# A transformer block with windowed attention and a gated feed-forward part: the last three attention units and the feed-forward part in a new order

## The chip, the cores and the metric

The kernel runs on one core of a Trainium2 chip. The metric is the device time of one execution in microseconds. The core has a matrix engine (PE; its weight loads are shown as PEld), a vector engine (DVE), an activation engine (ACT), a general engine (POOL) and a synchronisation engine (SP), which here issues nearly all DMAs. Each engine works through its own instructions in the order in which they were written; engines wait for one another by semaphores. An engine whose next instruction has to wait does nothing else meanwhile. Matrix products are accumulated in PSUM, which has eight banks of 128 x 512 fp32 values.

## The reference

The input x has 2048 rows of 512 columns. All data are fp32, and the kernel keeps fp32 accuracy by splitting most operands into a high and a low part and adding three products.

```python
mod = (silu(c) @ w_mod)                 # six rows of 512: sa, ca, ga, sb, cb, gb
h = layernorm(x) * (1 + ca) + sa
q, k, v = h @ wqkv                      # 32 heads of 16
scores = q k' / 4, masked to the 256 keys up to and with the query
x = x + ga * ((softmax(scores) @ v) @ wo)
h = layernorm(x) * (1 + cb) + sb
x = x + gb * ((silu(h @ w1) * (h @ w3)) @ w2)      # 1792 inner columns
```

## The kernel before, in words

**Units of the attention.** The 32 heads are taken in 8 groups of four, the 2048 rows in 4 blocks of 512. A unit u is one group and one block (`g, b = divmod(u, 4)`), so there are 32 units, and units 28 to 31 are the last group on the four blocks. The work on a unit has three parts. `unit_a` makes queries and keys: twelve products on PE (line 481), the evictions and splits (lines 487 to 499), and then three pairs of copies (`rows`, line 504) that put them into `ring`, from which scores are read. `unit_b` finds the row maxima: 16 score products (line 537), a masked maximum of each on DVE (`top`, line 544), two small DVE instructions that form `mr` from the maxima (`parts`, lines 552 and 554), a transposition on PE (`turn`, line 560), an eviction (line 565) and a copy of these rows into `ring` (line 569). `unit_c` makes the scores again, transposed and now with the maxima subtracted (line 855), and with one of several ways of masking: DVE merges (line 873) and POOL selections (line 883), or a second PE product (line 858). ACT takes the exponential (lines 867 and 876). The values are multiplied on PE (line 816), and the result is evicted (line 923) and stored in DRAM (line 926).

**After the attention.** The sums of the softmax are read back and inverted (`o_sums`, line 1196), the outputs are read back, scaled and split (`o_part`, lines 1214 to 1226), and `o_proj` multiplies by wo (line 1238), whose gated copy `load_wo` reads and splits with four casts on ACT and four subtractions on POOL (lines 1170, 1092 and 1093). Layer norm, transpositions and splits follow. The feed-forward part runs over two halves of the rows and seven pairs of 128-column blocks of the inner dimension; it uses a Strassen form with seven products in place of eight (line 1502, evictions at lines 1525 to 1546), splits its result (lines 1574 and 1577) and multiplies by w2 (line 1596), adding into x1 (line 1601). The weights of each pair are read by `load_w` (line 1296) into one of two sets of buffers and split into high and low parts on ACT and on DVE or POOL (lines 1092 and 1093). The split of wo, the weights and other splits share those two lines.

**What sets the order.** Up to time TS = 232, in a time scale of 8 per unit, the attention's operations are issued in the order of times written by hand (table X: an operation of a unit has the unit's start plus an offset). Operations from TS on are not issued in that order. They are given, with everything that follows the attention, to a list schedule (`Sched.deal`): these are mainly parts of the last three or four units, and all maxima work of the last unit. The list schedule goes through an imagined run. Each engine takes the ready operation with the smallest key; an operation is ready when those it depends on are done by the assumed lengths, not before its earliest time `est`. An engine may wait up to `LOOK[engine]` for an attention operation with a smaller key. It also hands out the eight banks. What it deals out is only the order of issue on each engine. Real dependences are kept by semaphores whatever the list assumes.

The assumed lengths of products by columns are `MM`. `PEM` and `PEA` are the extra time assumed until PE sees the result of ACT, DVE or POOL. The key of an attention operation is its hand time in microseconds plus an entry of `OFF`, less 1000; keys of other operations come from `K`. Of these, `wo` is the key of the wo loads, `n` the parts of a block that must be there before its first out-projection product, `o` the blocks' out-projection keys, `w` an addition to the keys of the weight loads, `fl` the key distance between pairs of the feed-forward part, `te` an anchor of its keys, and `by`, `be`, `su`, `sr` and `sw` name the engine, DVE or POOL, of each multiplication and subtraction. `wo`, `n` and the others are tuned numbers without another meaning.

A dependence is known to the list only if an operation states it by name. In the kernel before, scores of line 537 state the copies into `ring` only for units under 3 (`rq if u < 3 else []`): the copies of the last unit are issued by hand order before the list begins, so the list knows no operation that writes them. Earliest times of attention operations are set by

```python
o.att, o.est = True, max(0.0, us(t)) if t < TS + 4 else 0.0
```

so an operation with a hand time below 236 has an earliest time, and one above has 0 unless something that it depends on is later.

Of the kernel before, what the change touches and what calls it, by code (L numbers as in the profile page):

```python
# [55 lines left out]
NU = NQ * NB  # L56
# [9 lines left out]
MM = {512: 0.228, 384: 0.175, 320: 0.148, 256: 0.121, 128: 0.062}  # L66
# [221 lines left out]
def us(t):  # L288
# [13 lines left out]
PEA = 0.11  # L302
LOOK = dict(PE=0.17, ACT=0.56, DVE=0, POOL=0.48, SP=2.26, NIL=0.0)
# [3 lines left out]
OFF = (-32.4, 1.9, 31.8, -10.9, -41.3, -73.5, -71.5, -77.4, -34.7, -2.4, -93.5, -48.6, -6.7, -60.6, -31.7,  # L307
# [12 lines left out]
K = dict(off=OFF, be=(('DVE', 'DVE'), ('POOL', 'DVE'), ('POOL', 'DVE'), ('DVE', 'POOL'), ('POOL', 'POOL'),  # L320
         ('POOL', 'POOL'), ('POOL', 'DVE')), hr=2.131, de=2.436, wo=-5.452, x1=27.702, xb=-20.166, xl=-57.124,
         os=-30.972, ol=(-283.199, -169.889, -117.309, -7.043), pl=(-256.514, 34.596, -186.064, -72.727),
         pe=(-72.047, -51.379, -87.785, -5.093), o=(-209.809, 195.543, 313.113, 92.985), n=(3, 3, 3, 1),
         w0=41.734, l2=-43.794, f=5.37, fl=6.37, by=((('DVE', 'DVE'), ('POOL', 'DVE'), ('POOL', 'POOL'),
         ('DVE', 'POOL')), (('DVE', 'POOL'), ('DVE', 'DVE'), ('POOL', 'POOL'), ('POOL', 'DVE')), (('DVE',
         'DVE'), ('POOL', 'DVE'), ('DVE', 'DVE'), ('DVE', 'DVE')), (('DVE', 'DVE'), ('POOL', 'POOL'), ('DVE',
         'DVE'), ('DVE', 'DVE'))), w=-0.289, dn=1.69, ds=0.072, l3=-28.825, sw=('POOL', 'POOL', 'POOL',
         'POOL'), su=(('DVE', 'DVE', 'POOL', 'DVE'), ('POOL', 'POOL', 'DVE', 'POOL'), ('DVE', 'DVE', 'DVE',
# [3 lines left out]
def block_kernel(ctx: ExitStack, tc: tile.TileContext, x, wqk, wv, wo, w13, w2, c, crow, wmod, wmodt, out):  # L332
# [715 lines left out]
    for t, _, fn, kind, use in ops:  # L1048
        if t < TS and use and len(use) == 4 and use[3] in n:
            bk = use[1][0]  # L1050
            bk.i = ("st", "mx").index(use[3]) * 3 + n[use[3]] % 3
            bk.tile = take, bk.i
            n[use[3]] += 1
    sch = Sched(free, take, [], [])
    for t, _, fn, kind, use in last:
        reads, writes, occ = use[:3]
        eng = KINDS[kind][0]
# [585 lines left out]
    n = 0  # L1643
# [88 lines left out]
```

## Time and profile before

| quantity | us |
|---|---|
| median of three runs (lowest, highest) | 962.61 (962.32, 962.68) |
| time of the profiled execution | 960.54 |
| its span, from the first instruction to the last | 958.8 |
| PE busy | 940.2 |
| DVE busy | 730.2 |
| ACT busy | 549.0 |
| POOL busy | 531.6 |

The granted clock of PE is 0.988 on the mean over the span, where 1 is full speed. Products are pipelined, so the busy time of PE says where it was empty rather than how well it was used. In a timeline each row gives the start, the length, the engine, the line, the operation with what it writes and reads, the count of merged instructions and, in brackets, the idle time of that engine just before and what ended it. If several things were waited for, the one that ended last by the profile is named. Units are not named in the trace; a unit's work is recognised by its order.

### The profile page before, as it was taken

The numbers are of one execution on the slowest core, as the hardware profiler recorded it, in microseconds if no ns is written. First come the engines' busy times: TensorE is split into PE (matmuls) and PEld (weight loads), VectorE is DVE, ScalarE is ACT, GpSimd is POOL, SyncE is SP. The second block draws the span as 40 slices with busy tenths as digits, with TensorE's granted clock in tenths as the row PEclk, the third lists the DMA queues.
The fourth block names the chain that finished last, engine by engine and source line by source line (L and its number), as shares of the span: only waits on it lengthen the run. The fifth ranks groups of instructions, "written<-read, shape, count | busy, mean of one in ns | idle before, by whom it ended". The sixth has DMA issues, their size and how long they took to land.

```text
span 958.8 us, 17155 instructions
## 1 busy us (share of the span) xinstructions
PE 940.2 (98%) x5322; PEld 725.6 (76%) x5322; DVE 730.2 (76%) x2054; ACT 549.0 (57%) x1247; POOL 531.6 (55%) x738
## 2 busy tenths in 40 slices
PE   9999999999999999998899999999999999999998
PEld 6668767777777776775688778888888888888886
DVE  7976789898989898988667695766679765566545
ACT  3333787878787877776669854433446343433330
POOL 8611686878687777774643775268556422222320
PEclk7999999999999999999899999999999999999999
DMA  9611354444454444345793664576555532222102
GB/s 316 209 57 35 109 176 148 147 152 145 148 178 144 149 144 148 133 137 183 223 257 127 198 204 154 190 252 220 162 164 191 166 99 89 71 65 82 36 23 88
DMA packets 81702, 141.90 MB, mean 148 GB/s; under 512 B 10570, under 2 KB 23242, under 8 KB 81612
## 3 DMA queue, kind: packets, MB, share of 16 engines
q1 hardware_dynamic: 81180, 140.29, 45.4%
q8 instruction: 42, 0.69, 0.3%
q10 hardware_dynamic: 432, 0.53, 0.2%
q14 instruction: 48, 0.39, 0.1%
HBM read 85.99 MB, written 34.61 MB: 126 GB/s over the span
## 4 chain that ended last, share of the span: by engine, by line
PE 83%; DVE 6%; POOL 4%; DMA 3%; issue 2%; ACT 1%; SPq 0%; ACTq 0%; POOLq 0%; DVEq 0%
PE st L1502 10%; PE mx L1502 9%; PE pj L481 7%; PE st L855 7%; PE mx L537 7%; PE po L816 7%; PE mx L1596 6%; PE st L1596 5%; PE po L1502 4%; PE mx L655 3%; PE pj L1502 2%; PE mx L1238 2%; PE st L655 2%; PE po L1596 2%; PE pj L1596 2%
## 5 line engine op out<-in xcount | busy, mean ns | idle before, releaser
L544 DVE CUSTOM_DVE_ANT_0 junk<-mx,mskq 128x384 bf16<-128x384 f32 (+2 forms) x487 | 244.0, 527 | 29.4 <-PE mx L537 27.9
L855 PE MATMUL st<-ring 100*128 100x384 f32 (+2 forms) x488 | 148.2, 345 | 0.6 <-ACT pt L876 0.4
L537 PE MATMUL mx<-ring 96*128 96x384 f32 (+1 forms) x487 | 146.0, 341 | 1.9 <-DMA ring<-qk 1.0
L883 POOL TENSOR_SCALAR_AFFINE_SELECT pt<-pt 128x256 f32<-128x256 f32 x268 | 108.6, 408 | 62.1 <-ACT pt L876 51.9
L481 PE MATMUL pj<-hT,wq 128*128 128x512 f32 x384 | 133.9, 407 | 0.0
L876 ACT ACTIVATE pt<-st 128x256 f32<-128x256 f32 x263 | 94.2, 386 | 37.5 <-DVE st L873 29.2
L1546 POOL TENSOR_TENSOR t<-t,t 128x512 f32<-128x512 f32 x28 | 41.0, 1463 | 134.1 <-DVE t L1534 133.4
L537 PEld LDWEIGHTS mx<-ring 96*128 96x128 f32 x487 | 88.8, 189 | 32.4 <-DVE mt L544 21.7
L855 PEld LDWEIGHTS st<-ring 100*128 100x128 f32 x488 | 91.6, 191 | 18.6 <-issue 6.7
L816 PE MATMUL po<-pt,vS 128*17 128x256 f32 (+2 forms) x1408 | 97.6, 390 | 2.9 <-POOL pt L883 2.5
L499 POOL TENSOR_TENSOR qk<-qkr,qk 128x512 fp32r<-128x512 f32 x64 | 83.2, 1300 | 15.6 <-ACT qkr L487 15.3
L873 DVE COPY_PREDICATED st<-later,st 128x128 f32<-128x128 uint8 x263 | 71.0, 291 | 14.0 <-PE st L855 10.7
L481 PEld LDWEIGHTS pj<-hT,wq 128*128 128x128 f32 x384 | 71.6, 191 | 7.2 <-DVE hT L650 0.7
L1093 POOL TENSOR_TENSOR w<-w,w 128x512 fp32r<-128x512 f32 (+2 forms) x35 | 55.8, 1607 | 33.4 <-ACT w L1092 33.4
L816 PEld LDWEIGHTS po<-pt,vS 128*17 128x17 f32 x1408 | 32.7, 97 | 48.0 <-issue 20.8
L1534 DVE TENSOR_TENSOR t<-mx,t 128x512 f32<-128x512 f32 x54 | 36.9, 687 | 35.4 <-PE mx L1502 33.1
L1502 PE MATMUL st<-b,w 128*128 128x512 f32 x240 | 60.1, 390 | 1.1 <-ACT t L1541 1.1
L900 POOL TENSOR_SCALAR_AFFINE_SELECT sm<-sm 128x256 f32<-128x256 f32 x109 | 41.9, 406 | 27.2 <-ACT sm L890 23.1
L1502 PE MATMUL mx<-b,w 128*128 128x512 f32 x228 | 56.8, 390 | 0.1
L867 ACT ACTIVATE pt<-st 128x384 f32<-128x384 f32 (+2 forms) x109 | 45.7, 434 | 13.8 <-DVE st L863 12.3
L1502 PEld LDWEIGHTS st<-b,w 128*128 128x128 f32 x240 | 45.0, 188 | 10.9 <-ACT t L1541 1.5
L1534 DVE TENSOR_TENSOR t<-st,t 128x512 f32<-128x512 f32 x35 | 24.1, 688 | 36.2 <-PE st L1502 32.5
(339 smaller groups left out, 2139.1 us busy)
## 6 DMA issues: line engine op xcount, KB each, us to landing
ring<-qk SPq DMA_DIRECT2D x192, 128.0 KB
o_dr<-os SPq DMA_DIRECT2D x32, 256.0 KB
w<-wsum SPq DMA_DIRECT2D x14, 512.0 KB
w<-w2g SPq DMA_DIRECT2D x14, 512.0 KB
jb<-in_w SPq DMA_DIRECT2D x24, 256.0 KB
wraw<-in_w SPq DMA_DIRECT2D x7, 768.0 KB
w<-wraw SPq DMA_DIRECT2D x14, 384.0 KB
e<-in_w SPq DMA_DIRECT2D x18, 256.0 KB
```

What stands on the lines that cost most here:

```text
L481: nc.tensor.matmul(v["ps"], WQ[g][w][:, n // 3], hTp(i, n // 3, b * BT, BT), start=(n == 0), stop=(n == 3 * KC - 1))
L499: nc.gpsimd.tensor_tensor(out=v[n], in0=v["raw"], in1=v[1].bitcast(F32), op=ALU.subtract)
L537: nc.tensor.matmul(v[i][:, :n], queries(NS, a, gq, 1), keys(NS, hh, a, k0, gq + 1 - k0), start=True, stop=True)
L544: nc.vector.tensor_tensor_reduce(out=junk[:, :n], in0=v[i][:, :n], in1=mskq[:, 3 * P - n:], scale=1.0, scalar=-3e38, op0=ALU.add, op1=ALU. ...
L816: nc.tensor.matmul(po[32 * i:32 * i + DH + 1, qb * P:(qb + nq) * P], vS[:, kb, 4 * g + i], pts[i // 2][:, i % 2, c0:c0 + nq], start=first, ...
L855: nc.tensor.matmul(ps[:, :nq], keys(NM, hh, a, kb, 1), queries(NM, a, kb, nq), start=True, stop=not plus)
L873: nc.vector.copy_predicated(ps[:, 0], later, ps[:, 2])
L876: nc.scalar.activation(pt_of(j, a)[:, hh, :2], v[j, a, hh][:, :2], AF.Exp, scale=SCALE)
L883: nc.gpsimd.affine_select(out=pt[:, :, 2 * m], in_=pt[:, :, 0], **w)
L1502: nc.tensor.matmul(ps(bk), WT[s, n][w][:, col], BB[t, k][r], start=start and c == 0, stop=stop and c == 5, skip_group_check=True)
L1534: return nc.vector.tensor_add(o, x, y)
L1596: nc.tensor.matmul(ps(bk), tiles[hk + (h,)][:, i * P:(i + 1) * P], w2_of(last, y, f), start=(m == 0), stop=(m == 5))
```

## The change

The change has four parts. First, a place-holder operation on the queue NIL, which issues nothing, is added to the list: it writes the name `("keys", 31)` and has the earliest time 1.9. Scores of line 537 of units from 3 on now read `("keys", u)`, so that the list holds the last unit's scores back until 1.9 us after its start; the other units' names have no writer and hold nothing back. The index into `OFF` is moved by one, since the place-holder comes first. Second, the assumed product lengths are set anew, and so are `PEA` and the entries PE, ACT, POOL and SP of `LOOK`. Third, all 206 entries of `OFF` are new. Fourth, all numbers of `K` are new, with the engines of many multiplications and subtractions. All four splits of wo stay on POOL.

```diff
-MM = {512: 0.228, 384: 0.175, 320: 0.148, 256: 0.121, 128: 0.062}
+MM = {512: 0.2303, 384: 0.177, 256: 0.124, 128: 0.07}
...
-PEA = 0.11
-LOOK = dict(PE=0.17, ACT=0.56, DVE=0, POOL=0.48, SP=2.26, NIL=0.0)
+PEA = 0.05
+LOOK = dict(PE=0, ACT=0.57, DVE=0.0, POOL=1.87, SP=0.93, NIL=0.0)
...
-OFF = (-32.4, 1.9, 31.8, -10.9, -41.3, -73.5, -71.5, -77.4, -34.7, -2.4, -93.5, -48.6, -6.7, -60.6, -31.7,
...
+OFF = (-49.5, -12.1, -22.4, -33.6, -56.0, -86.7, -88.5, -93.2, -17.6, 12.1, -94.0, -56.8, -33.7, -64.4, -78.4,
...
-         ('POOL', 'POOL'), ('POOL', 'DVE')), hr=2.131, de=2.436, wo=-5.452, x1=27.702, xb=-20.166, xl=-57.124,
-         os=-30.972, ol=(-283.199, -169.889, -117.309, -7.043), pl=(-256.514, 34.596, -186.064, -72.727),
-         pe=(-72.047, -51.379, -87.785, -5.093), o=(-209.809, 195.543, 313.113, 92.985), n=(3, 3, 3, 1),
-         w0=41.734, l2=-43.794, f=5.37, fl=6.37, by=((('DVE', 'DVE'), ('POOL', 'DVE'), ('POOL', 'POOL'),
...
-         'DVE'), ('DVE', 'DVE'))), w=-0.289, dn=1.69, ds=0.072, l3=-28.825, sw=('POOL', 'POOL', 'POOL',
...
+         ('DVE', 'POOL'), ('DVE', 'POOL')), hr=21.549, de=1.941, wo=-21.362, x1=28.573, xb=-29.268,
+         xl=-116.162, os=-27.898, ol=(-190.566, -166.456, -108.194, -61.649), pl=(-220.589, 37.55, -68.89,
+         -99.113), pe=(-60.146, -15.682, -95.487, -36.215), o=(-234.765, 94.893, 305.699, 215.681), n=(2, 1,
+         1, 2), w0=44.978, l2=-60.842, f=17.513, fl=5.731, by=((('POOL', 'POOL'), ('POOL', 'DVE'), ('POOL',
...
+         'DVE'), ('DVE', 'DVE'), ('DVE', 'DVE'))), w=20.278, dn=1.62, ds=-0.071, l3=-47.032, sw=('POOL',
...
-            at(t0 + y["mx"][i], lambda i=i: scores(i, bk[i]), "scores", (rq if u < 3 else [], [bk[i]], MM[n], "mx"))
+            at(t0 + y["mx"][i], lambda i=i: scores(i, bk[i]), "scores", (rq if u < 3 else [("keys", u)], [bk[i]], MM[n], "mx"))
...
     sch = Sched(free, take, [], [])
+    sch.op("NIL", lambda: None, 0.0, 0.0, [], [("keys", NU - 1)]).est = 1.9
...
-        o = sch.op(eng, fn, occ, us(t) + K["off"][len(sch.ops)] - 1000, reads, writes, mode=int(kind == "values"))
+        o = sch.op(eng, fn, occ, us(t) + K["off"][len(sch.ops) - 1] - 1000, reads, writes, mode=int(kind == "values"))
```

More of the change, by code (lines that the diff above doesn't have):

```diff
@@ new lines @@
+OFF = (-49.5, -12.1, -22.4, -33.6, -56.0, -86.7, -88.5, -93.2, -17.6, 12.1, -94.0, -56.8, -33.7, -64.4, -78.4,
[13 rows of a table added]
+K = dict(off=OFF, be=(('DVE', 'DVE'), ('POOL', 'POOL'), ('DVE', 'POOL'), ('POOL', 'DVE'), ('DVE', 'POOL'),
+         ('DVE', 'POOL'), ('DVE', 'POOL')), hr=21.549, de=1.941, wo=-21.362, x1=28.573, xb=-29.268,
+         xl=-116.162, os=-27.898, ol=(-190.566, -166.456, -108.194, -61.649), pl=(-220.589, 37.55, -68.89,
+         -99.113), pe=(-60.146, -15.682, -95.487, -36.215), o=(-234.765, 94.893, 305.699, 215.681), n=(2, 1,
+         1, 2), w0=44.978, l2=-60.842, f=17.513, fl=5.731, by=((('POOL', 'POOL'), ('POOL', 'DVE'), ('POOL',
+         'DVE'), ('DVE', 'DVE')), (('POOL', 'DVE'), ('POOL', 'DVE'), ('DVE', 'POOL'), ('DVE', 'DVE')),
+         (('DVE', 'DVE'), ('DVE', 'POOL'), ('POOL', 'DVE'), ('DVE', 'DVE')), (('POOL', 'DVE'), ('POOL',
+         'DVE'), ('DVE', 'DVE'), ('DVE', 'DVE'))), w=20.278, dn=1.62, ds=-0.071, l3=-47.032, sw=('POOL',
+         'POOL', 'POOL', 'POOL'), su=(('DVE', 'POOL', 'DVE', 'DVE'), ('DVE', 'DVE', 'POOL', 'POOL'), ('DVE',
+         'DVE', 'POOL', 'DVE')), sr=(('POOL', 'DVE', 'POOL', 'DVE', 'DVE', 'DVE', 'DVE', 'POOL', 'POOL',
+         'DVE', 'DVE'), ('DVE', 'DVE', 'DVE', 'DVE', 'POOL', 'DVE', 'DVE', 'DVE', 'POOL', 'POOL', 'POOL')),
+         te=45.488)
```

6 lines of the change are left out of this document (removed), and 25 rows, old and new, of the table OFF.

## The prediction

> **What bounds the kernel now.** I read the page first, then the busy time in stretches of 24 us, and then the two stretches that were not full.
>
> ```profile
> span 958.8 us, 17155 instructions
> PE 940.2 (98%) x5322; PEld 725.6 (76%) x5322; DVE 730.2 (76%) x2054; ACT 549.0 (57%) x1247; POOL 531.6 (55%) x738
> ...
> 432.00:456.00 24.00, 19.91 (x139) 12.11 (x131) 21.05 (x85) 14.45 (x40) 11.62 (x21) 0.93 0.60 181
> 456.00:480.00 24.00, 21.86 (x182) 15.60 (x186) 14.56 (x36) 17.28 (x48) 15.01 (x24) 0.86 0.77 227
> 528.00:552.00 24.00, 22.88 (x109) 18.81 (x108) 14.88 (x31) 20.45 (x35) 18.64 (x16) 1.00 0.62 203
> 576.00:600.00 24.00, 24.00 (x110) 19.86 (x109) 13.11 (x19) 9.45 (x15) 11.70 (x14) 1.00 0.49 154
> 600.00:624.00 24.00, 24.00 (x113) 19.95 (x112) 16.30 (x23) 11.00 (x18) 7.41 (x9) 1.00 0.55 187
> 912.00:936.00 24.00, 24.00 (x106) 19.70 (x106) 12.30 (x19) 8.10 (x14) 5.14 (x4) 1.00 0.07 23
> 936.00:960.00 24.00, 18.75 (x83) 15.06 (x81) 11.51 (x18) 1.27 (x2) 0.00 (x0) 1.00 0.23 88
> ```
>
> The columns of a stretch are its length, the busy time of PE, PEld, DVE, ACT and POOL, the granted clock, the DMA share and GB/s. TensorE (PE) is the bound: full at clock 1.00 in a feed-forward stretch such as 600 to 624. It loses 4.09 us of idle at 432 to 456, 2.14 at 456 to 480 and 1.12 at 528 to 552; the last stretch holds the closing additions and stores. The clock falls below 1.00 only in the two stretches around 456, where the order written by hand ends and the list schedule begins. So I looked at those microsecond by microsecond, with the same columns:
>
> ```profile
> 441.00:442.00 1.00, 0.75 (x5) 0.40 (x3) 1.00 (x5) 0.70 (x4) 0.93 (x3) 1.00 0.57 197
> 442.00:443.00 1.00, 0.00 (x0) 0.00 (x0) 1.00 (x3) 0.09 (x1) 0.95 (x3) 1.00 0.63 195
> 443.00:444.00 1.00, 0.00 (x0) 0.01 (x1) 0.06 (x1) 1.00 (x3) 0.57 (x2) 1.00 0.26 76
> 444.00:445.00 1.00, 0.98 (x4) 0.80 (x4) 0.54 (x2) 0.08 (x1) 0.24 (x1) 0.70 0.78 236
> 447.00:448.00 1.00, 1.00 (x10) 0.43 (x2) 0.37 (x4) 0.00 (x0) 0.00 (x0) 0.60 0.69 172
> 455.00:456.00 1.00, 0.00 (x0) 0.00 (x0) 1.00 (x5) 0.00 (x0) 0.95 (x2) 1.00 1.17 254
> 459.00:460.00 1.00, 1.00 (x4) 1.00 (x5) 1.00 (x2) 0.27 (x1) 1.00 (x1) 0.50 0.43 95
> 464.00:465.00 1.00, 1.00 (x5) 1.00 (x5) 0.50 (x2) 1.00 (x4) 0.69 (x2) 0.56 0.65 207
> ```
>
> There are two holes in PE, and a half clock behind each. A clock of 0.70 at 444 to 445 and 0.60 at 447 to 448 puts the first half-clock time at about 444.4 to 447.8, 3.4 us, of which 1.7 are lost; the second one runs to about 464.9, and from 459.0, where PE is busy again, 5.9 us at half speed lose 2.95.
>
> Next, who ends the holes, from the timeline:
>
> ```profile
> 439.85 1.92 SPq L504 DMA_DIRECT2D ring<-qk  x3
> 441.20 0.55 PE L855 MATMUL st<-ring 100*128 100x384 f32 x2
> 444.02 0.41 PE L537 MATMUL st<-ring 96*128 96x384 f32 x1 [2.27 <-ACT pt L876]
> 444.46 0.56 DVE L544 CUSTOM_DVE_ANT_0 junk<-st,mskq 128x384 bf16<-128x384 f32 x1 [1.40 <-PE st L537]
> 446.46 0.55 DVE L544 CUSTOM_DVE_ANT_0 junk<-pj,mskq 128x384 bf16<-128x384 f32 x1
> 447.06 0.18 DVE L552 SCALAR_TENSOR_TENSOR mr<-mt,zero 128x16 fp32r<-128x16 f32 x1
> 447.27 0.17 DVE L554 SCALAR_TENSOR_TENSOR mr<-mt,mr 128x16 fp32r<-128x16 f32 x1
> ...
> 456.40 2.49 POOL L1093 TENSOR_TENSOR wo<-wo,wo 128x512 fp32r<-128x512 f32 x2
> 456.48 0.84 PE L816 MATMUL po<-pt,vS 128*17 128x384 f32 x8 [1.81 <-POOL pt L883]
> 456.92 0.79 DVE L552 SCALAR_TENSOR_TENSOR mr<-mt,zero 128x16 fp32r<-128x16 f32 x1
> 457.74 1.18 DVE L554 SCALAR_TENSOR_TENSOR mr<-mt,mr 128x16 fp32r<-128x16 f32 x1
> 458.98 0.40 PE L560 MATMUL mx<-ident,mr 128*32 128x128 f32 x1 [1.65 <-DVE mr L554]
> ```
>
> The first hole (2.27 us) ends with a score of line 537. In the kernel before, a score of the last unit from the seventh on has the earliest time 0 in the list schedule and reads nothing, so the schedule may put it at its very start. The trace shows five row maxima (L544) from 444.46 to 446.46 and then the two mr instructions of the last but one unit. That unit had only three maxima left by its times (scores 13 to 15), so two of the five belong to the last unit, and a score of it stood at the head of PE. Its rows cannot have been there: their last copy was issued at about 441.2 and ended issuing at 441.77, and the chain of waits gives 2.29 us to such a copy:
>
> ```profile
> 439.26 2.29 DMA ring<-qk
> ```
>
> 441.2 + 2.29 is 443.5, near the start at 444.02. The ACT instruction that the wait is put down to fits too, so the DMA as its cause is my reading, not the profile's. The second hole is a chain on DVE: all sixteen maxima of the last unit, the two mr instructions, then the transposition on PE at 458.98, whose rows the remaining scores need.
>
> **The change part by part.** No instruction of computation is added or removed; what is new is the order on every engine from about 441 on, and which of DVE and POOL does some splits. The new operation on the queue "NIL" issues nothing.
>
> *The landing time.* The list's time 0 lies near 441.1 (its first PE score, planned at 0.30, is the second of the pair at 441.20), so 1.9 means 443.0, half a microsecond before the estimate 443.5. PE can now first take the two open scores of the last but one unit, and DVE their maxima and a third one: three maxima of 0.50 each (the first and the fifth start at 444.46 and 446.46: 2.00 / 4), 1.5 us, of which 1.4 fit into the 1.40 that DVE waited ahead of 444.46. The DVE chain to the transposition, 444.46 to 458.98, thus gets 1.4 shorter. The bounds are 0 (the new order puts another late operation at the head) and 2.27 (nothing waits).
>
> *The two mr instructions* took 0.79 + 1.18 = 1.97 at 456.92 and only 0.18 + 0.17 = 0.35 at 447.06. In the slow case the POOL was at a subtraction for wo from 456.40 to 458.89. The change moves wo from key -5.5 to -21.4, ahead of more of its rivals, and there is room for it:
>
> ```profile
> 448.66 0.60 ACT L923 ACTIVATE os<-po 128x512 f32<-128x512 f32 x1 [4.58 <-PE po L816]
> 450.45 0.88 POOL L883 TENSOR_SCALAR_AFFINE_SELECT pt<-pt 128x256 f32<-128x256 f32 x2 [6.21 <-ACT pt L876]
> 452.37 2.18 ACT L1092 ACTIVATE wo<-wo 128x512 fp32r<-128x512 f32 x4
> 453.07 2.52 POOL L1093 TENSOR_TENSOR wo<-wo,wo 128x512 fp32r<-128x512 f32 x2 [1.75 <-ACT wo L1092]
> ```
>
> ACT idles 4.58 us and POOL 6.21 before 450.5, while the four casts and four subtractions need 2.18 and 2.52 + 2.49. I take it that they move up and the mr pair falls to 0.35: a gain of 1.6. Bounds: 0, and 1.6. The Trainium skill, SBUF — State Buffer, section "SBUF: two separate sides", says that DVE with two SBUF inputs and GpSimd exclude each other from a shared port pair for a whole instruction; the slow pair agrees. By that rule the 1.6 is won only if no such POOL instruction is running just then; if one is, the sum stands at 1.4. The list schedule itself counts no such conflict for the mr pair, so a repetition of the slow rows is a rival below.
>
> *The first half clock* (1.7) should go with the first hole, but PE then merely reaches the second hole earlier, since DVE sets that one's end: I count 0 for it, with 1.7 as the bound. The same holds for the idle time of the first hole itself.
>
> *The values' wait* (1.81 at 456.48, behind POOL's wo work) and *the second half clock* (2.95) I keep at 0: the new order of keys does not say what PE finds to do at 455. If out-projection products are ready then (the parts waited for before the first product of a block go from 3, 3, 3, 1 to 2, 1, 1, 2), both go: bound 4.76. The other side of starting a block on fewer parts is that PE, which issues in order, stands behind a part that lands late; one landing like the 2.29 above is the bound, -2.3.
>
> *Product lengths, look-ahead, feed-forward keys.* Lengths go from 0.228 to 0.2303 for 512 columns; that costs no time by itself, only other choices. From 576 to 936 PE is full before but for 0.06 us at most in a stretch (first and last stretch above), so only a loss is possible there, priced with the rivals; up to it, the waits behind line 1541 could go:
>
> ```profile
> PE st L1502 <- ACT t L1541: 1.4, 2, 1.1
> ```
>
> I count 0, bound 1.4.
>
> *Sum.* 1.4 + 1.6 = 3.0 earlier at the transposition; PE is busy from there on but for about a microsecond, so the end moves with it. The profiled execution took 960.54 us, 1.74 above its span; 960.54 - 3.0 = 957.5. The three timed runs have the median 962.61, 2.07 above the profiled one, so the forecast is 962.61 - 3.0 = 959.6. With every bound on the good side the sum is 1.4 + 1.6 + 4.76 + 1.4 + 1.7 = 10.9, hence 951.7.
>
> The Trainium skill, TensorE: Matmul & The Clock Gate, section "HAM oscillation — how this bites in real kernels", speaks of PE idle gaps above about 3.4 us as those that cost the clock. Here 2.27 us and 1.81 + 1.65 us were enough, so I go by the trace; by the rule the two half clocks would not have come from these holes, and the good bound would shrink by 4.65 to 956.4.
>
> **The rivals.** *More is won:* the transposition comes 3.0 earlier and the second hole is filled as well. Then the 1.81 and the 2.95 go too: 3.0 + 4.76 = 7.8, time 954.8. For it: DMA, ACT and POOL have room around 448. Against it: the four wo subtractions are not the last step, loads of o and of the sums come behind them in a DMA share of 0.9 to 1.17.
>
> *The POOL still blocks:* only the 1.4 comes, time 961.2, within what a measurement of this kernel can tell from no change (about 0.2%, 1.9 us). For it: the list schedule does not count the conflict, and the slow pair above shows it. Against it: wo is moved away from there.
>
> *Weights late, the slower side.* The key of a pair's weight loads moves from 0.3 below to 20.3 above its base, so loads and splits now yield to much other work. The narrowest lead that I found before:
>
> ```profile
> 669.03 2.87 POOL L1093 TENSOR_TENSOR o<-o,o 128x1024 fp32r<-128x1024 f32 x1
> 681.94 1.53 PE L1502 MATMUL pj<-b,o 128*128 128x512 f32 x6
> ```
>
> Split done at 671.90, first product at 681.94: 10.0 us. A key is a rank, not a time, but if loads came later by more than 10.0, PE would stand for the rest. Midway between 10 and the full shift of 20.6 that is 5.3 idle and about 1.7 of half clock, less the 3.0 won: 4.0 slower, 966.6. Against it: POOL and ACT are at 31% and 46% in the stretch 600 to 624.
>
> *The change does not do what it says:* if the first hole came from the ACT instruction alone, the 1.4 falls and the 1.6 may stay: 961.0, counted with no change.
>
> **How the numbers follow.** Forecast 0.34; more 0.25; no difference (the POOL blocks, or the rows were not the cause) 0.19; slower, by late weights or by a part that lands late, 0.22. The first two are faster by over 0.2%: 0.59. The predicted time is 959.6. Below 952.5 lies only what needs nearly all good bounds at once (0.07), above 966.5 the upper half of the late-weight case (0.11); the range is 952.5 to 966.5. The faster cases alone span 952.5 to 960.7.
>
> **What will show it.** Right: no hole above 1 us near 442 to 444, scores of the last unit after about 443.5, an mr pair of 0.35 us and the transposition of line 560 near 456, clock 1.00 at 444 to 448. The forecast rather than "more" holds if PE still idles over 2 us ahead of that transposition with a half clock behind it. Wrong: a hole of the same size at the boundary that ends on ACT or DVE; the mr pair again above 1 us beside a POOL subtraction; idle time of PE ahead of line 1502 or 1238 after 480, ended by a weight split or a load; a longer end than the last four microseconds of before.

## The result, and the profile after

The changed kernel took 957.1 us in the median of four executions (956.48 to 957.99), the kernel before beside it 962.64 (962.32 to 965.44): ratio 0.9935, interval 0.9909 to 0.9960. In a later comparison on another chip it was 956.23 against 964.64, ratio 0.9924 (0.9904 to 0.9944). It is faster by 5.5 to 8.4 us; 3.0 was forecast. The profiled execution took 957.99 us, 1.7 above its span of 956.3.

The profiles start unequal. The last two products of the order written by hand (line 855 before, 857 after; both kernels issue the same up to there) begin at 441.20 before and at 442.85 after. So I count from these two products, "the last pair", to the end of the span: 517.6 us before, 513.4 after, 4.2 less.

The changed kernel's stretches of 24 us; columns as in the prediction:

```profile
432.00:456.00 24.00, 21.88 (x157) 12.59 (x155) 23.35 (x93) 15.42 (x42) 14.42 (x25) 1.00 0.60 178
456.00:480.00 24.00, 22.47 (x188) 15.41 (x185) 12.83 (x39) 18.44 (x50) 14.95 (x24) 0.93 0.89 253
528.00:552.00 24.00, 23.54 (x112) 19.35 (x111) 18.21 (x32) 21.25 (x35) 18.59 (x15) 1.00 0.61 208
576.00:600.00 24.00, 24.00 (x108) 19.78 (x107) 13.63 (x20) 10.31 (x17) 12.65 (x14) 1.00 0.52 165
```

PE's idle time in the first three went from 4.09 + 2.14 + 1.12 = 7.35 to 2.12 + 1.53 + 0.46 = 4.11, and the clock in the first two from 0.93 and 0.86 to 1.00 and 0.93. The feed-forward part is as full as it was. The timeline of the changed kernel:

```profile
442.85 0.55 PE L857 MATMUL st<-ring 100*128 100x384 f32 x2
443.41 0.44 PE L539 MATMUL st<-ring 96*128 96x384 f32 x1
443.96 1.27 PE L818 MATMUL po<-pt,vS 128*17 128x384 f32 x16
...
453.39 0.62 PE L539 MATMUL mx<-ring 96*128 96x384 f32 x2 [0.30 <-ACT pt L869]
454.42 0.45 PE L539 MATMUL mx<-ring 96*128 96x384 f32 x1 [0.40 <-ACT pt L878]
455.29 1.28 POOL L1096 TENSOR_TENSOR wo<-wo,wo 128x512 fp32r<-128x512 f32 x1
455.37 0.84 PE L818 MATMUL po<-pt,vS 128*17 128x384 f32 x8 [0.33 <-POOL pt L885]
458.64 1.28 POOL L1229 TENSOR_TENSOR qk<-qk,qk 128x512 f32<-128x512 f32 x1
459.59 0.36 DVE L554 SCALAR_TENSOR_TENSOR mr<-mt,zero 128x16 fp32r<-128x16 f32 x1
459.99 0.32 DVE L556 SCALAR_TENSOR_TENSOR mr<-mt,mr 128x16 fp32r<-128x16 f32 x1
460.48 0.27 PE L562 MATMUL mx<-ident,mr 128*32 128x128 f32 x1
464.62 2.25 PE L818 MATMUL po<-pt,vS 128*17 128x384 f32 x32 [1.13 <-ACT os L925]
534.43 1.66 PE L1505 MATMUL po<-b,w 128*128 128x512 f32 x6 [0.46 <-ACT t L1544]
```

The first hole (2.27 us) is gone: PE goes from the last pair to open scores and to values. Of the second hole (1.81 + 1.65) there are left three waits of 0.30, 0.40 and 0.33. The longest wait of PE behind the last pair is now 1.13 us, at 464.62, ended by ACT. The pair of mr instructions takes 0.68 in place of 1.97. But the last unit's transposition comes 17.6 us after the last pair (460.48 - 442.85); before it was 17.8 (458.98 - 441.20). It has hardly moved, and the end is 4.2 earlier.

One table for all runs. Fourth column: span less the start of the last pair. Fifth: median of the timed executions. The runs stand in four groups, each beside the kernel before on one chip. The four medians of the first row belong, in this order, to changed, to e_later to e_wodve, to e_fill1 to e_undo, and to the last four.

| kernel | last pair at | span | from it to the end | median | ratio to before |
|---|---|---|---|---|---|
| before | 441.20 | 958.8 | 517.6 | 962.64 / 963.08 / 961.74 / 964.64 | |
| changed | 442.85 | 956.3 | 513.4 | 957.1 | 0.9935 (0.9909 to 0.9960) |
| e_later | 442.72 | 957.5 | 514.8 | 958.25 | 0.9946 (0.9925 to 0.9967) |
| e_ahead | 441.81 | 963.1 | 521.3 | 964.62 | 1.0014 (0.9996 to 1.0032) |
| e_both | 442.47 | 959.3 | 516.8 | 960.49 | 0.9969 (0.9952 to 0.9985) |
| e_wodve | 442.42 | 964.5 | 522.1 | 963.82 | 1.0008 (0.9991 to 1.0024) |
| e_fill1 | 443.45 | 959.2 | 515.8 | 960.45 | 0.9988 (0.9974 to 1.0001) |
| e_fill2 | 440.74 | 958.1 | 517.4 | 961.14 | 0.9995 (0.9982 to 1.0007) |
| e_later_fill2 | 442.69 | 957.3 | 514.6 | 958.74 | 0.9968 (0.9951 to 0.9985) |
| e_undo | 440.67 | 955.3 | 514.6 | 959.34 | 0.9982 (0.9961 to 1.0004) |
| e_after2 | 440.68 | 954.3 | 513.6 | 956.23 | 0.9924 (0.9904 to 0.9944) |
| e_undo_fill1 | 443.23 | 956.4 | 513.2 | 957.87 | 0.9939 (0.9917 to 0.9961) |
| e_after_fill | 442.01 | 954.5 | 512.5 | 956.19 | 0.9919 (0.9900 to 0.9939) |
| e_later2 | 441.90 | 956.9 | 515.0 | 958.23 | 0.9941 (0.9921 to 0.9961) |

The last pair alone varies by 2.8 us between executions that are the same up to there, so small differences of medians are weak and the fourth column is the better one, for the one execution that it shows.

### The profile page after: what moved, and what is told of

Same layout as the page of the kernel before. It is cut to its first block, busy times and chain, and to the rows that moved or that the text cites. A ratio compares the mean times of both kernels' runs of the same rounds, so it can differ in the third digit from the quotient of the medians.

```text
span 956.3 us, 17149 instructions
## 1 busy us (share of the span) xinstructions
PE 940.2 (98%) x5322; PEld 724.5 (76%) x5322; DVE 738.7 (77%) x2055; ACT 549.4 (57%) x1247; POOL 521.6 (55%) x737
## 4 chain that ended last, share of the span: by engine, by line
PE 83%; POOL 5%; DMA 4%; DVE 3%; issue 2%; ACT 2%; SPq 0%; POOLq 0%; ACTq 0%; DVEq 0%
PE st L1505 12%; PE mx L1505 10%; PE pj L483 7%; PE mx L539 7%; PE st L857 7%; PE mx L1599 7%; PE po L818 6%; PE st L1599 5%; PE pj L1505 3%; PE mx L657 3%; PE po L1505 3%; PE po L1599 2%; PE pj L1599 2%; POOL pt L885 2%; POOL qk L501 2%
## 5 line engine op out<-in xcount | busy, mean ns | idle before, releaser
L546 DVE CUSTOM_DVE_ANT_0 junk<-mx,mskq 128x384 bf16<-128x384 f32 (+1 forms) x483 | 242.1, 527 | 30.7 <-PE mx L539 29.2
L857 PE MATMUL st<-ring 100*128 100x384 f32 (+2 forms) x484 | 145.9, 343 | 0.6 <-ACT pt L878 0.4
L878 ACT ACTIVATE pt<-st 128x256 f32<-128x256 f32 x255 | 91.4, 387 | 37.6 <-DVE st L875 30.3
L1096 POOL TENSOR_TENSOR w<-w,w 128x512 fp32r<-128x512 f32 (+2 forms) x35 | 51.6, 1485 | 57.4 <-ACT w L1095 57.4
L1537 DVE TENSOR_TENSOR t<-st,t 128x512 f32<-128x512 f32 x55 | 37.8, 690 | 49.4 <-PE st L1505 37.7
L875 DVE COPY_PREDICATED st<-later,st 128x128 f32<-128x128 uint8 x255 | 68.7, 291 | 7.0 <-PE st L857 3.7
L869 ACT ACTIVATE pt<-st 128x384 f32<-128x384 f32 (+2 forms) x113 | 47.1, 433 | 13.7 <-DVE st L865 12.6
L1505 PE MATMUL mx<-b,w 128*128 128x512 f32 x204 | 51.4, 390 | 0.0
L1577 ACT ACTIVATE qkr<-g 128x512 fp32r<-128x512 f32 x13 | 8.2, 632 | 66.4 <-DVE g L1533 66.4
```

Source lines behind the costliest of these rows:

```text
L546: nc.vector.tensor_tensor_reduce(out=junk[:, :n], in0=v[i][:, :n], in1=mskq[:, 3 * P - n:], scale=1.0, scalar=-3e38, op0=ALU.add, op1=ALU. ...
L857: nc.tensor.matmul(ps[:, :nq], keys(NM, hh, a, kb, 1), queries(NM, a, kb, nq), start=True, stop=not plus)
L875: nc.vector.copy_predicated(ps[:, 0], later, ps[:, 2])
L878: nc.scalar.activation(pt_of(j, a)[:, hh, :2], v[j, a, hh][:, :2], AF.Exp, scale=SCALE)
L1096: sch.op(eng, lambda: on_eng(eng).tensor_tensor(out=lo(), in0=src(), in1=hi().bitcast(F32), op=ALU.subtract), tt(eng, n), key, kl + kh, kl ...
L1505: nc.tensor.matmul(ps(bk), WT[s, n][w][:, col], BB[t, k][r], start=start and c == 0, stop=stop and c == 5, skip_group_check=True)
```

## The experiments

### One part at a time

Four kernels change the order of the kernel before by hand, after the list has dealt it out, and leave its numbers alone. In the code, of which only parts are shown, `find` looks up an operation by its kind and by what it reads or writes, and `move(o, ref)` puts it behind `ref`, or ahead of it with `False`. In e_later only the last unit's two early scores (the seventh and the eleventh) and their maxima stand later:

```diff
...
+    ref = find("values", ("pv", 28, 2))
+    mr = find("parts", ("mr", NU - 2))
+    for i in (6, 10):
+        top = find("top", ("mt", NU - 1, i))
+        sc = find("scores", top.bank[0])
+        move(sc, ref)
+        move(top, mr)
+        ref, mr = sc, top
...
```

> The kernel before with one piece of its order changed: the two scores of the last unit that stood at the head of the list, and their two maxima, come later (the scores behind the first two groups of value products, the maxima behind the mr pair of the last but one unit). Everything else keeps its order and its engines. Theory A (the prediction's: the last unit's transposition at 458.98 sets the end, holes ahead of it are absorbed): the first hole of 2.27 us goes, the half clock at 444.4 to 447.8 goes, DVE loses its 1.40 of waiting, the transposition comes 1.4 earlier relative to the boundary, and the time falls by 1.4. Theory B (what counts is only whether PE, in order, stands behind something late while other work is ready): the first hole goes too, but PE then stands the longer in front of the same transposition; time lower by 0 to 1.4. If the rows of the last unit were not the cause of the first hole, it stays at about 2.3 us behind ACT. If holes are simply additive, 2.27 + 1.7 = 4.0 come off.

```profile
442.72 0.54 PE L856 MATMUL st<-ring 100*128 100x384 f32 x2
...
445.53 0.41 PE L538 MATMUL st<-ring 96*128 96x384 f32 x1 [0.71 <-ACT pt L877]
...
455.49 1.24 DVE L553 SCALAR_TENSOR_TENSOR mr<-mt,zero 128x16 fp32r<-128x16 f32 x1
455.51 1.01 PE L817 MATMUL po<-pt,vS 128*17 128x384 f32 x8 [2.43 <-POOL pt L884]
456.76 1.18 DVE L555 SCALAR_TENSOR_TENSOR mr<-mt,mr 128x16 fp32r<-128x16 f32 x1
458.00 0.40 PE L561 MATMUL mx<-ident,mr 128*32 128x128 f32 x1 [1.47 <-DVE mr L555]
```

This timeline still has the second hole (2.43 + 1.47) and the slow mr pair. Yet moving two scores gives 0.9946, 4.8 us in the medians and so most of what the change gives. The moved score, behind the values, still waits 0.71 us. The transposition comes 15.3 us after the last pair (458.00 - 442.72) in place of 17.8, which is 2.5 earlier; 1.4 was my term for it. The end comes 2.8 earlier.

In e_ahead six scores of units 29 and 30, which stood behind the last transposition, stand ahead of it and of the values that waited; e_both has both moves.

```diff
...
+    ref = find("values", ("pv", 29, 1))
+    turn = find("turn", ("mr", NU - 1), False)
+    late = [o for o in lst[lst.index(turn):] if o.tag == "scores"][:6]
+    for o in late:
+        move(o, ref, False)
...
```

> The kernel before with another piece of its order changed: the six scores of the last but one and the third last unit that stood behind the last unit's transposition on PE are put ahead of the value products and of that transposition. DVE, ACT, POOL and SP keep their order. Theory A: the transposition stays at 17.2 us behind the boundary reciprocal of DVE (458.98 - 441.73), so the end stays: 0, at most 0.5 either way. Theory B: the 1.81 + 1.65 us of idle PE at 454.7 to 459.0 is filled with about 1.9 us of scores, the share of busy PE in that stretch rises from about a quarter to over a half, the half clock to 464.9 (2.95 us lost) goes: 3.5 to 4.8 us faster.

> The kernel before with both pieces: the last unit's two scores and maxima later, and the six other scores ahead of the transposition. Theory A: 1.4 faster. Theory B: both half clocks and most of both holes go, 5 to 6 us faster, about what the change brings (5.5). If the two holes only pass idle time on to each other, no more than the better of the two alone.

The move gained nothing: e_ahead takes the time of the kernel before (the 521.3 of its one profile goes with a longer half clock, see below), and e_both is slower than e_later. The timeline of e_both shows why there:

```profile
456.54 0.66 PE L856 MATMUL st<-ring 100*128 100x384 f32 x1 [3.71 <-DMA ring<-mT]
```

The first of the six stood 3.71 us for the rows of unit 30, which had not landed, with everything on PE behind it. e_both's last pair is followed by 516.8 us, 2.0 more than e_later's.

In e_wodve the last two subtractions for wo are done by DVE, behind the mr pair, so that POOL has none of them beside it:

```diff
...
+    mr = find("parts", ("mr", NU - 1))
+    for k in (2, 3):
+        o = next(o for o in lst if o.alt and ("wo", 0, k) in o.uses[0])
+        o.fn = o.alt
+        move(o, mr)
+        mr = o
...
```

> The kernel before with the last two of the four subtractions for wo moved from POOL to DVE, behind the last unit's mr pair. Both theories: POOL is no longer at a subtraction while the mr pair runs, so the pair falls from 1.97 us to 0.35 unless another POOL instruction with SBUF reads takes its place; the transposition comes up to 1.6 earlier. Theory A: the time falls by 1.6. Theory B: PE's second wait (1.65) shrinks, but the first part of the second hole (1.81, POOL's mask behind the wo work) and the half clock stay: 0 to 1.6 faster.

```profile
442.42 0.54 PE L856 MATMUL st<-ring 100*128 100x384 f32 x2
...
445.17 0.66 PE L538 MATMUL st<-ring 96*128 96x384 f32 x1 [2.21 <-ACT pt L877]
...
460.19 1.27 POOL L1229 TENSOR_TENSOR qk<-qk,qk 128x512 f32<-128x512 f32 x1
460.70 0.79 DVE L553 SCALAR_TENSOR_TENSOR mr<-mt,zero 128x16 fp32r<-128x16 f32 x1
461.42 1.26 POOL L1229 TENSOR_TENSOR wq<-wq,wq 128x512 f32<-128x512 f32 x1
461.53 1.19 DVE L555 SCALAR_TENSOR_TENSOR mr<-mt,mr 128x16 fp32r<-128x16 f32 x1
462.77 0.40 PE L561 MATMUL mx<-ident,mr 128*32 128x128 f32 x1 [1.66 <-DVE mr L555]
```

The pair is as slow as before (0.79 + 1.19), because POOL's next work, two multiplications of line 1229 that scale the outputs (line 1226 of the kernel before), moved into the place. So the test did not take away what it was to take away: it is not wo alone that slows the pair; a POOL multiplication of the same size beside it does so as well. In the changed kernel wo's last subtraction ends at 456.57, and a multiplication of line 1229 at 459.92, within the first mr instruction (459.59 to 459.95); the pair falls where POOL is nearly done.

This run showed something else. Up to the subtractions its order is that of the kernel before, and its transposition comes 20.4 us after the last pair, 2.6 later than in the profile before. The clock in stretches of 3.41 us tells them apart; first the kernel before, then e_wodve:

```profile
440.99:444.40 3.41, 1.14 (x7) 0.82 (x6) 2.07 (x7) 1.89 (x7) 2.70 (x7) 1.00 0.51 159
444.40:447.81 3.41, 3.41 (x21) 1.21 (x20) 2.91 (x12) 0.00 (x0) 0.00 (x0) 0.50 0.84 261
```

```profile
440.98:444.39 3.41, 1.86 (x8) 0.98 (x6) 3.29 (x12) 2.21 (x8) 3.04 (x7) 1.00 0.59 193
444.39:447.80 3.41, 2.63 (x12) 1.47 (x16) 1.85 (x7) 0.90 (x3) 0.81 (x2) 0.50 0.76 215
447.80:451.21 3.41, 3.41 (x24) 1.55 (x17) 1.55 (x8) 0.58 (x2) 0.00 (x0) 0.50 0.83 252
451.21:454.62 3.41, 3.41 (x17) 2.18 (x17) 2.47 (x7) 1.19 (x5) 0.81 (x2) 0.50 0.76 261
454.62:458.03 3.41, 3.41 (x29) 2.11 (x29) 2.90 (x13) 2.74 (x6) 1.16 (x1) 1.00 0.67 190
```

The same hole is followed by a half clock of one such stretch in the first and of three in the second, 10.2 us. In the first the hole lies wholly in one stretch and the next is full; in the second it reaches into the next stretch. e_ahead shows three stretches as well, with its hole reaching over a border; e_fill2 and e_undo, below, one, with the hole inside one stretch. So in five profiles out of five the length goes with where the hole lies against the borders. That where it lies is what makes it long is my reading; I had no means to set it. From the last pair to the end e_wodve took 522.1 us, 4.5 more than the profile before. Its second half clock is longer too, from 461.4 to 471.7 in place of 458.0 to 464.9, so the 4.5 is not the price of the first one alone.

### Products that do nothing useful

To part the price of a hole from that of the half clock behind it, these kernels put extra products of 256 columns in the holes, whose result the next real product overwrites. No real work moves. e_fill1 has 18 in the first hole, e_fill2 16 and 8 ahead of the two waits of the second, and e_later_fill2 has the second set on top of e_later.

```diff
...
+    def fill(o, bk, n):
+        real = o.fn
+
+        def go():
+            for _ in range(n):
+                nc.tensor.matmul(ps(bk)[:, :2 * P], identr, mskr[:, :2], start=True, stop=True)
+            real()
+        o.fn = go
+    top = find("top", ("mt", NU - 1, 6))
+    fill(find("scores", top.bank[0]), top.bank[0], 18)
...
```

> The kernel before, with extra work alone: 18 products of 256 columns ahead of the last unit's first score of the list, whose result that score overwrites in its bank. They take about 1.9 us and stand where TensorE otherwise idles 2.27 us for the rows. Nothing real is moved, and the score itself can start no earlier. Theory 'the half clock is the price of the first hole': the idle time of real work stays, but the half clock behind it goes, so the time falls by what that half clock lost, 1.7 us (3.4 us long) to 5 us (10 us long): 958 to 961 against about 963. Theory 'the vector engine's chain sets the second hole' (my prediction's view, in which this half clock was counted 0): the transposition comes when it came, about 17.2 us after the first reciprocal, and the time stays within 1 us. Theory 'the late start of the real products is the price': also no change.

```profile
443.45 0.56 PE L856 MATMUL st<-ring 100*128 100x384 f32 x2
444.01 2.41 PE L1693 MATMUL st<-mskr,identr 128*128 128x256 f32 x18
446.26 0.34 PE L538 MATMUL st<-ring 96*128 96x384 f32 x1
...
459.59 0.40 PE L561 MATMUL mx<-ident,mr 128*32 128x128 f32 x1 [1.65 <-DVE mr L555]
```

```profile
445.67:449.08 3.41, 3.41 (x37) 1.93 (x35) 2.44 (x10) 0.67 (x2) 0.76 (x2) 1.00 0.83 241
```

The real score starts 2.8 us after the last pair, as before (444.02 - 441.20), but the stretch behind it runs at clock 1.00, and the transposition comes 16.1 after the last pair in place of 17.8, the end 515.8 in place of 517.6. Up to the transposition the half clock alone costs 1.6, nearly all of the 1.7 that it loses. (The 1.8 at the end has something else in it: the second half clock is one stretch shorter here, 459.3 to 462.7 in place of 458.0 to 464.9. The next run shows how little that is worth.) So the vector engine's chain is not a clock of its own: while PE was slow, DVE waited for scores, as the prediction's own row for 447 to 448 shows (DVE busy 0.37 of 1.00 beside PE at 1.00 and clock 0.60). In the medians the gain is 1.3 us with an interval that touches none (0.9974 to 1.0001), so the reading rests on the profile.

> The kernel before, with extra work alone in the second hole: 16 products of 256 columns ahead of the values that waited 1.81 us, and 8 ahead of the last transposition that waited 1.65 us, all into the bank that the transposition overwrites. Theory 'half clock': the second half clock (5.9 us long behind the hole, 2.95 us lost) goes, and the time falls by 2 to 3 us to 960 to 961 against about 963; the first hole and its half clock stay. Rival 'the products push real work back': no gain, or up to 1 us lost.

```profile
440.74 0.55 PE L856 MATMUL st<-ring 100*128 100x384 f32 x2
...
458.54 0.28 PE L561 MATMUL mx<-ident,mr 128*32 128x128 f32 x1 [0.53 <-DVE mr L555]
...
460.82 0.44 PE L856 MATMUL st<-ring 100*128 100x384 f32 x1 [0.41 <-ACT pt L877]
```

The second half clock, of which I had counted 2.95 as lost, is gone, and the end comes 517.4 after the last pair, 0.2 earlier than before. The transposition comes 17.8 after the last pair, as before, so the extra products pushed nothing back ahead of it. PE is faster behind the transposition and then waits for ACT. So the second half clock lay beside another limit and cost next to nothing. In the medians the gain is 0.6 us, with an interval that touches none (0.9982 to 1.0007).

> The two edits together: the last unit's two scores and their maxima later, as in the run of that name (958.25 us), and the extra products in the second hole. If each hole costs its own half clock and they add up: 958.2 less 2 to 3, 955 to 956.5, which would be at or below the changed kernel (957.1). If the second hole is set by the vector engine and the extra products only delay it: 958 or more.

It agrees: 514.6 from the last pair to the end, 514.8 without the extra products, though the clock stayed at 1.00 in the whole region. My expectation of 955 to 956.5 fell. This profile also names what the moved score waits for:

```profile
442.69 0.54 PE L856 MATMUL st<-ring 100*128 100x384 f32 x2
...
445.54 0.41 PE L538 MATMUL st<-ring 96*128 96x384 f32 x1 [0.76 <-DMA ring<-qk]
```

It is the copy of the rows into `ring`, and the wait ends 2.85 us after the last pair. In e_later the same score starts 2.81 us after it (445.53 - 442.72), though the wait is put down to ACT there.

### Undoing one part, and the changed kernel with extra products

e_undo is the changed kernel with the last unit's seventh and eleventh scores put back behind the first score of the list; all else keeps the new order. e_undo_fill1 adds 17 extra products ahead of them.

```diff
...
+    ref = next(o for o in lst if o.tag == "scores")
+    for i in (6, 10):
+        top = find("top", ("mt", NU - 1, i))
+        sc = find("scores", top.bank[0])
+        move(sc, ref)
+        ref = sc
...
```

> The changed kernel with one thing undone: the last unit's scores 6 and 10 stand at the head of the list's order on TensorE again, as the old list placed them, all else in the new order. Theory 'the place of these scores is the change': the hole of about 2.3 us and its half clock come back, 957.1 + 2.3 + 1.7 to 5 = 961 to 964. Theory 'the rest of the new order brings the gain': the time stays within 1.5 us of 957.1.

```profile
440.67 0.54 PE L858 MATMUL st<-ring 100*128 100x384 f32 x2
443.36 0.48 PE L540 MATMUL mx<-ring 96*128 96x384 f32 x1 [2.15 <-DVE st L876]
```

```profile
440.17:443.58 3.41, 1.26 (x6) 0.91 (x7) 3.41 (x11) 2.17 (x8) 2.81 (x8) 1.00 0.49 156
443.58:446.99 3.41, 3.41 (x20) 1.21 (x19) 1.61 (x8) 0.00 (x0) 0.13 (x1) 0.50 0.90 266
```

The hole and a half clock are back, and most of the gain is gone: 0.9982. 959.34 lies between what the two theories expected (961 to 964, or within 1.5 of 957.1). Its ten executions lie between 957.06 and 963.54, the profiled one being the fastest, with the short half clock. They fall into two groups: six with a mean granted clock of 0.990 to 0.993 took 957.06 to 959.57, four with 0.984 or 0.985 took 961.55 to 963.54. From the last pair on the profile ends only 1.2 later than the changed kernel's, which has a half clock at another place (below) that this one lacks. The hole ends 2.7 us after the last pair; it was 2.8 in the kernel before, in e_wodve and in e_ahead. The instruction named as the releaser is one of DVE here and one of ACT there, while the distance is the same. That fits the landing of the rows, which the profile of e_later_fill2 names at the same distance.

> The changed kernel with the last unit's scores 6 and 10 back at the head of the list's order (that gave 959.34 us, spread from 957.1 to 963.5), and 17 extra products of 256 columns ahead of the first of them, whose result it overwrites. The hole of 2.15 us then is busy, but with nothing useful. Theory 'half clock of chance length': the half clock behind the hole is what made the spread, 1.7 us lost in some executions and 5.1 in others; with the extra products the spread shrinks to about 3 us and the median comes to within 1 us of the changed kernel beside it, or below what the scores at the head gave by 1.7 to 3 us. Theory 'late start': the useless products save nothing; the time stays 2 us or more above the changed kernel's.

```profile
443.23 0.54 PE L858 MATMUL st<-ring 100*128 100x384 f32 x2
443.60 2.18 PE L1702 MATMUL mx<-mskr,identr 128*128 128x256 f32 x17
445.77 0.41 PE L540 MATMUL mx<-ring 96*128 96x384 f32 x1
```

From the last pair to the end it takes 513.2 us, as the changed kernel does (513.4, 513.6), and the ratio is 0.9939. With nothing but useless products ahead of the same late score, most of the loss is taken back. But the clock stays at 1.00 in the whole region, so this profile also lacks the half clock of the changed kernel. Beside e_after_fill (next), which has no half clock either and starts the scores behind the last pair at once, the end comes 0.7 later (513.2 against 512.5), and the median is 1.7 higher (957.87 against 956.19). So the late start of the real scores cost less here than the 2.2 us that PE spends on useless products. The spread was to shrink to 3 us; it was 5.3 (955.15 to 960.49), so not all of it came from this half clock. The median lies 1.6 above the changed kernel beside it, between what the two theories said, and with six executions of each this is not told from nothing.

e_after_fill puts two extra products ahead of each of six scores of the last unit, shortly ahead of the three waits of the changed kernel. e_after2 is the changed kernel again, e_later2 is e_later again, all on one chip.

```diff
...
+    scs = [o for o in lst if o.tag == "scores"]
+    for o in scs[18:24]:
+        fill(o, o.bank[0], 2)
...
```

> The changed kernel with 12 extra products of 256 columns (about 1.3 us of work whose result is overwritten), two ahead of each of six scores of the last unit just before the three waits at 453.4, 454.4 and 455.4 us (1.03 us in sum), so that TensorE has no stretch with less than nine tenths of work there. If the half clock at 456.3 to 459.7 (1.7 us lost) comes from that stretch: 1.5 us faster than the changed kernel beside it, less up to 0.3 us for the surplus. If the extra products push real work back: equal to it, or up to 1.3 us slower.

The changed kernel, in stretches of 3.41 us, and then e_after_fill:

```profile
452.86:456.27 3.41, 2.38 (x15) 0.86 (x14) 3.23 (x12) 1.39 (x4) 3.04 (x4) 1.00 0.89 238
456.27:459.68 3.41, 3.41 (x12) 3.29 (x13) 2.52 (x12) 1.82 (x5) 2.57 (x3) 0.50 1.06 322
...
463.10:466.51 3.41, 2.28 (x40) 0.77 (x32) 0.68 (x2) 3.41 (x9) 2.14 (x6) 1.00 0.81 211
```

```profile
451.30:454.71 3.41, 3.31 (x24) 2.57 (x26) 3.03 (x11) 1.91 (x4) 2.43 (x4) 1.00 1.00 286
454.71:458.12 3.41, 3.37 (x21) 1.96 (x13) 3.35 (x16) 1.73 (x5) 3.08 (x3) 1.00 0.85 254
```

The extra products keep the clock, and the profile is 0.9 us better from the last pair on (512.5). The medians do not show it: 956.19 against 956.23.

> The changed kernel unaltered, on the same chip as the three kernels beside it, so that they can be set against it directly. 956.5 to 958 by its first runs; if the chip matters as much as the other runs suggest, its distance to the kernel before may lie between 3 and 6 us.

> The kernel before with nothing but the last unit's two scores and their two maxima moved later, once more, beside the changed kernel on the same chip. Theory 'the place of these two scores is the change': within 1.5 us of the changed kernel. Theory 'the rest of the new order brings half of it': 2.5 us or more above it.

On this chip the kernel before has 964.64, e_later2 958.23 and the changed kernel 956.23. The distance of the changed kernel, 8.4, is more than the 3 to 6 that I expected. Two scores moved later give 6.4 of it; the other 2.0, between what the two theories expected of e_later2, come with the rest of the new order. The distance varies with the kernel before. Of its executions in the last three groups, the 21 with a mean granted clock of 0.984 took 963.96 to 966.18 us, the 34 with 0.988 or more 958.98 to 963.80. The former are 10 of 26 beside e_later, 5 of 31 beside e_fill1 and 6 of 11 here. So it is time at half clock that spreads them; the mean does not say behind which hole.

## Why the prediction was right and where it failed

The time was in the range and the sign was right, and the likeliest case had the right place: the first hole. The gain was underestimated, and by a step that I had written down as zero.

*Landing time: right in place, wrong in make-up.* The hole went, and with the two scores at the head of the new order it came back (e_undo). "1.4 shorter" is 2.5 in e_later, above my bound of 2.27. But 1.6 is what e_fill1 gets from the half clock alone, because the slow PE had also delayed the scores that DVE waits for. By that, 0.9 is left for the hole itself, less than 1.4.

*"I count 0 for it", the first half clock: the step that failed.* The reason given was that DVE sets the end of the second hole. e_fill1 takes away this half clock and moves no real work, and the transposition comes 1.6 earlier and the end 1.8. DVE was waiting for PE in just that time; the row that I quoted for the clock (447.00) says so in its DVE column, and I read only its PE and clock columns. The bound, 1.7, was also too low: I took it from one execution, and the same hole can be followed by three stretches at half speed. The kernel before ran between 958.98 and 966.18 in all executions here, the changed kernel between 955.27 and 958.55. The profile before, 960.54, is one of the shorter executions; that is why the medians differ by more than the two profiles.

*"The end moves with it", with the transposition: wrong.* In the changed kernel it comes 17.6 after the last pair, not 3.0 earlier than 17.8, since the new list puts a dozen scores of units 29 and 30 and other work ahead of it. In the old order it does move so: in e_later the transposition is 2.5 earlier and the end 2.8, in e_fill1 1.6 and 1.8. What counts for the end is how long PE is empty or slow where its work is ready. By the terms that the runs measured: PE's idle time from the last pair to 940 us is 7.23 (498.80 - 491.57) before and 3.79 (497.15 - 493.36) after, so 3.4 less; the first half clock 1.8 less, the second 0.2 less, a new one behind the three small waits 0.9 more: 4.5. PE's last product ends at 954.76 before and at 951.86 after, 4.5 earlier counted from the last pair. The stretch from there to the end is 4.4 us in place of 4.0, a longer end as named among the signs of being wrong, and so 4.2 are left. The prices of the half clocks were measured on other orders, so that the sum comes out supports the account and does not prove it.

*The mr pair: right in size, half right in cause.* 0.68 in place of 1.97 is 1.3 of the 1.6. wo did move up: its last subtraction ends 13.7 us after the last pair (456.57 - 442.85), before it was 17.7 (458.89 - 441.20). But e_wodve shows that with wo gone the next POOL instruction, a multiplication, takes its place. (The rule that I cited from the Trainium skill, SBUF — State Buffer, section "SBUF: two separate sides", names any such instruction of POOL; the 0.79 + 1.19 beside line 1229 agrees.) e_later has most of the gain with the pair at 2.42, so most of the time did not come from this term. Whether the rest did was not run. That the forecast's 3.0 comes near the measured gain is in part luck: 1.6 of it stood for a step that no run shows to have paid, and the first half clock, which did pay, stood at 0.

*"I keep at 0" the values' wait and the second half clock, with 4.76 as the bound.* The values' wait shrank to 0.33; the second half clock was worth 0.2, not 2.95. The rival "more is won" (954.8) priced it at full; 957.1 lies midway between its time and the forecast's, and the way was neither's.

*Line 1541* gave 1.12 - 0.46 = 0.7 of a bound of 1.4. *Late weights* did not come: 576 to 600 is full, and so is every stretch of 24 us from there to 936. *"The POOL still blocks"* falls with the pair at 0.68, *"does not do what it says"* with the first hole.

*What stays open.* The new numbers apart from the landing time (lengths, `LOOK`, `OFF`, `K`) were not run one by one. Whether the landing time with the old numbers would do the same wasn't tried. That the rows' DMA ends the hole is named by one profile, e_later_fill2, for the moved score; for the hole itself it is inferred from the same distance. The 2.0 us that the changed kernel gains beyond e_later2 were not taken apart.

## What to carry to other kernels

A hole in PE of some 2 us has two prices: the late start of the work behind it, which was less than its length here, and half of one or of three stretches of 3.41 us, if work is ready behind it. Filling it with useless products parts the two, without moving anything. A half clock costs next to nothing where the work behind it waits for something else (0.2 us in e_fill2), so before it is priced, look at what PE would do next at full speed. An engine that "sets the end" of a wait may itself have been fed by the slow one: look at its idle time in the same rows. And in an order dealt out by a list, give the list every transfer that it cannot see.

## What the runs showed of the hardware

The clock changes only at borders 3.41 us apart: in the sets of rows above it is 0.50 or 1.00 in whole stretches, and 10.2 us is three of them. The Trainium skill, TensorE: Matmul & The Clock Gate, section Part 1: The HAM clock gate (the "warmup" mystery), gives a free-running window of 3413 ns, and the traces agree. The rule of the same page, section "HAM oscillation — how this bites in real kernels", that it takes idle gaps above about 3.4 us does not hold here: a gap of 2.27 us cost the clock, and in the changed kernel so did a stretch busy for 2.38 of 3.41 us whose longest gap is 0.40. Nor does the busy share alone decide: the stretch from 463.10 was busy for 2.28 and no half clock followed.

That one hole is followed by 3.4 us at half speed in one execution and by 10.2 in another I had not expected. In five profiles the short one goes with a full stretch right behind the border. Why in the long case a second full stretch still ran at half speed isn't explained by any run here.
